# A softmax denominator's constant, its reciprocal and its column of ones: three small moves in a fused attention and soft-MoE kernel

## The chip, the cores and the metric

The kernel runs on one core of one Trainium2 chip. The metric is the device time of one execution in microseconds (us); times of several executions are given by their median. The profile is of one further execution, taken by the hardware profiler.

The engines named below are PE (TensorE, matrix products and transposes), DVE (VectorE), ACT (ScalarE), POOL (GpSimd, which also issues most of the loads) and SP (SyncE, which issues the loads of v and the stores).

## The reference

The first half is attention with one extra term in the softmax denominator, the second a soft mixture of experts on its output. Only the first half matters here:

```python
scores = scale * np.matmul(q, k.transpose(0, 1, 3, 2))
m = np.max(scores, axis=-1, keepdims=True)
e = np.exp(scores - m)
attn = e / (np.sum(e, axis=-1, keepdims=True) + np.exp(-m) + 1e-09)
return np.matmul(attn, v).astype(np.float32)
```

There are 8 batches, 12 heads, 448 positions and 64 numbers per head. `np.exp(-m)` is the sink term, one number for each row of scores, and `1e-09` the constant of this document's title. The result, with the heads laid side by side, is the input `x` (3584 x 768) of the mixture: logits `x @ phi`, a softmax over the rows for the slots' inputs, two layers of weights per expert, and a softmax over the slots to mix their outputs back into every row.

## The kernel before, in words

The attention is cut into 24 **units**, u = 0 to 23; a unit is two batches by two heads (a head pair), and six units make up one pair of batches. A unit is worked in 7 **steps** of 64 positions. Everything is placed on one clock of steps, n = 7u + s: a function `at(n, where, f)` (L679) notes what is to be issued at step n, and the loop at L726 issues it. Within a step the order is: what is noted as "small", the score tile of step n, "value", the transposed score tile of step n - 10, "end", "load". The program is issued in exactly this order, engine by engine; nothing reorders it later. Each engine works through its own list in order and waits on semaphores for what others make.

What a unit does, with its place on the clock (n = 7u):

- `stage_S` (L220), steps n to n + 6: PE writes a score tile into PSUM (L226, in the last step L230) and DVE takes its row maxima (L234, 128 x 896 numbers). These reductions fill most of DVE's time.
- `stage_T` (L208), step n + 5: PE transposes q and k of the next unit, DVE copies them out (L217).
- `stage_MT` (L236), step n + 7: the maxima are transposed on PE (L238), copied by ACT (L240), ACT makes the sink terms `em` (L242), and POOL writes the maxima in the form that PE can subtract, in two parts (L246, L252).
- `stage_ST` (L257), steps n + 10 to n + 16: PE makes the transposed scores with the maxima subtracted (L262, L267), ACT the exponential (L271).
- `stage_V` (L274), step n + 9: POOL converts v to bf16 (L276) and writes a 1.0 beside each value (L278), so that the product with v also yields the row sums. The target is one of two buffers, by the parity of u.
- `stage_AV` (L281), steps n + 13 to n + 18: PE multiplies with v (L297). `stage_AVout`, step n + 19: ACT copies the product out (L308, L311) into `xu`, of which there is one buffer.
- `stage_den` (L314), step n + 20: POOL adds row sum and sink term (L317) and then 1e-9 (L318).
- `stage_N` (L321), step n + 22, "small": DVE takes the reciprocal (L324), POOL multiplies (L326). For u = 22 it is step n + 21 and both are on DVE; unit 23 has a function of its own, `stage_last`, that adds its own 1e-9.
- `stage_X` (L369), step n + 26: PE transposes the result (L378), DVE copies it out (L379).

So the reciprocal of unit u stands in DVE's list between the first and the second reduction of unit u + 3 (steps 0 and 1 of that unit). In the same stretch POOL's list has: the loads of q and k (L124, four DMAs) and of weights (L155, one DMA, in units 9, 13 and 16 two), issued at step 5 of a unit; L317 and L318 at step 6; L246 and L252 at step 7, which is step 0 of the next unit; L326 at its step 1; L276 and L278 at its step 2. `mixture` (L391) puts further work between, once per six units: among it POOL's subtraction `gate_max` (L487), which waits for DVE, and its multiplication `gate_out` (L499).

Score tiles, transposed score tiles and all transposes share one ring of three PSUM slots (`slot`, L115; 496 tiles in all). A tile usually takes the slot that was taken three tiles ago, and PE waits until its reader, DVE or ACT, is done with it. So the transposed score tile of a step usually waits for DVE's reduction of the step before, and a score tile for ACT's exponential two steps back. At three places the build gives a transposed score tile the slot of the transposed score tile of the step before, two tiles back: in unit 10 at its steps 2 and 3 and in unit 14 at its step 2, counted by the score tiles that are made then.

Of the kernel before, what the change touches and what calls it, by code (L numbers as in the profile page):

```python
# [13 lines left out]
ALU = mybir.AluOpType  # L14
# [9 lines left out]
def kernel(  # L24
# [10 lines left out]
    nc = tc.nc  # L35

    B, H, S, D = q.shape
# [10 lines left out]
    U = BP * HP  # L48
# [9 lines left out]
    small = ctx.enter_context(tc.tile_pool(name="small", bufs=2))  # L58
# [30 lines left out]
    def buf(name, i):  # L89
        o, n, bufs = parts[name]  # L90
        return block[:, ds(o + (i % bufs) * n, n)]

    def xbuf(u):
        return block[:, ds(xbuf_at((u + 4) % (HP + 1)), N2)]
# [20 lines left out]
    def slot(shape, dtype=F32):  # L115
        return ring.tile(shape, dtype, tag="r", name="ps")
# [11 lines left out]
    def load_qk(u):  # L128

        for i, (src, name) in enumerate(((q, "qr"), (k, "kr"))):  # L130
            t_ = buf(name, 0) if u else wres[:, WRES - 1, ts(i, N2)]
            RAW[u, name] = load(u, t_.rearrange("p (h n) -> p h n", h=2), src, nc.gpsimd)

    def load_v(u):
        t_ = block[:, ds(parts["vr" if u < U - 1 else "qr"][0], 2 * N2)].bitcast(F32).rearrange("p (h n) -> p h n", h=2)
        RAW[u, "vr"] = load(u, t_, v, nc.sync if u else nc.gpsimd)
# [71 lines left out]
    def stage_T(u, name):  # L208

        ps = slot([128, 2, S], BF16)  # L210
        r = RAW.pop((u, name))
        for t in range(TB):
            for h in range(2):
                nc.tensor.transpose(ps[ds(h * D, D), :, ds(t * P, P)],  # L214
                                    r[:, h, ds(t * D, D)], ident)
        t_ = buf(f"qk{u % 3}", 0)[:, ts(int(name == "kr"), N2)].rearrange("p (b n) -> p b n", b=2)
        nc.vector.tensor_copy(t_, ps)  # L217
        (QT if name == "qr" else KT)[u] = t_
# [17 lines left out]
    def stage_MT(u):  # L236
        ps = slot([128, 128], BF16)
        nc.tensor.transpose(ps, M[u % 2], ident)  # L238
        mt = small.tile([128, 128], BF16, tag="mt", name="mt", bufs=1)
        (nc.scalar.copy if u < U - 1 else nc.vector.tensor_copy)(mt, ps)  # L240
        em = small.tile([128, 2, TB], F32, tag="em", name="em", bufs=3)
        nc.scalar.activation(em, M[u % 2].rearrange("p (h r) -> p h r", h=2)[:, :, ds(0, TB)],  # L242
                             AF.Exp, scale=-scale)
        EM[u] = em
        md = buf(f"md{u % 2}", 0).rearrange("p (b n) -> p b n", b=2)
        nc.gpsimd.tensor_tensor(  # L246
            md[:, :, ds(0, C3 * 128)].rearrange("p b (c n) -> p b c n", c=C3),
            mt.unsqueeze(1).unsqueeze(1).broadcast_to([128, 2, C3, 128]),
            nmask[:, ds(0, 2 * C3)].rearrange("p (b c) -> p b c", b=2).unsqueeze(3)
                 .broadcast_to([128, 2, C3, 128]),  # L250
            op=ALU.mult)
        nc.gpsimd.tensor_tensor(  # L252
            md[:, :, ds(C3 * 128, P)], mt.rearrange("p (b n) -> p b n", b=2),
            nmask[:, ds(2 * C3, 1)].unsqueeze(2).broadcast_to([128, 2, P]), op=ALU.mult)
        MD[u] = md

    def stage_ST(u, t):  # L257
        ps = slot([128, 2, 512])
        for b in range(2):
            for h in range(2):  # L260
                hs = ds(h * D, D)
                nc.tensor.matmul(ps[ds(b * P, P), h, ds(0, S)], ones[hs, :], MD[u][hs, b, :],  # L262
                                 start=True, stop=False)
        for b in range(2):
            for h in range(2):
                hs = ds(h * D, D)
                nc.tensor.matmul(ps[ds(b * P, P), h, ds(0, S)],  # L267
                                 KT[u][hs, b, ds(t * P, P)], QT[u][hs, b, :],
                                 start=False, stop=True)
        et = buf("et", u * TB + t).rearrange("p (h n) -> p h n", h=2)  # L270
        nc.scalar.activation(et, ps[:, :, ds(0, S)], AF.Exp, scale=scale)  # L271
        ET[u, t] = et

    def stage_V(u):  # L274
        t_ = buf(f"v6{5 + u % 2}", 0).rearrange("p (h t e) -> p h t e", h=2, e=66)
        nc.gpsimd.tensor_copy(t_[:, :, :, ds(0, D)],  # L276
                              RAW.pop((u, "vr")).rearrange("p h (t d) -> p h t d", t=TB))
        nc.gpsimd.memset(t_[:, :, :, ds(D, 1)], 1.0)  # L278
        V65[u] = t_

    def stage_AV(u, ts_, part):  # L281

        for t in ts_:
            if t == 0 and part == 0:
                AV[u] = pav.tile([128, 2, 512], F32, tag="av", name="av")
            av, et = AV[u], ET[u, t]
            for h in range(2):
                for c in (range(C3) if part == 0 else (C3,)):  # L290
                    for b in range(2):
                        bs = ds(b * P, P)
                        if c < C3:
                            o, w = av[:, b, ds((h * C3 + c) * 65, 65)], 128
                        else:
                            o, w = av[bs, h, ds(2 * C3 * 65, 65)], P
                        nc.tensor.matmul(o, et[bs, h, ds(c * 128, w)],  # L297
                                         V65[u][bs, h, t, ds(0, 65)],
                                         start=(t == 0 and h == 0 and c == 0),
                                         stop=(t == TB - 1), skip_group_check=True)  # L300
            if part == 1:
                ET.pop((u, t))

    def stage_AVout(u):
        av = AV.pop(u)
        xu = buf("xu", 0).bitcast(F32).rearrange("p (h s e) -> p h s e", h=2, e=65)
        copy = nc.scalar.copy if u < U - 2 else nc.vector.tensor_copy
        copy(  # L308
            xu[:, :, ds(0, 2 * C3), :].rearrange("p h (b c) e -> p b h (c e)", b=2),
            av[:, :, ds(0, 2 * C3 * 65)].rearrange("p b (h e) -> p b h e", h=2))  # L310
        copy(xu[:, :, TB - 1, :], av[:, :, ds(2 * C3 * 65, 65)])  # L311
        XU[u] = xu

    def stage_den(u):  # L314
        xu = XU[u]
        den = small.tile([128, 2, TB], F32, tag="den", name="den")
        nc.gpsimd.tensor_tensor(den, xu[:, :, :, D], EM.pop(u), op=ALU.add)  # L317
        nc.gpsimd.tensor_scalar(den, den, 1e-9, None, op0=ALU.add)  # L318
        DEN[u] = den

    def stage_N(u):  # L321
        xv = XU.pop(u)
        rec = small.tile([128, 2, TB], F32, tag="rec", name="rec", bufs=1)
        nc.vector.reciprocal(rec, DEN.pop(u))  # L324
        x = xbuf(u).rearrange("p (s n) -> p s n", s=TB)
        (nc.gpsimd if u < U - 2 else nc.vector).tensor_tensor(  # L326
            x.rearrange("p s (h d) -> p h s d", h=2), xv[:, :, :, ds(0, D)],
            rec.unsqueeze(3).broadcast_to([128, 2, TB, D]), op=ALU.mult)
        X[u] = x
# [349 lines left out]
    def at(n, where, f):  # L679
        plan.setdefault((n, where), []).append(f)  # L680

    for u in range(U):
        n = u * TB
        if u + 1 < U:
            at(n + 5, "value", lambda u=u: [stage_T(u + 1, name) for name in ("qr", "kr")])
        if u + 2 < U:
            at(n + 5, "load", lambda u=u: load_qk(u + 2))
        at(n + 7, "value" if u < U - 1 else "small", lambda u=u: stage_MT(u))
        at(n + (9 if u < U - 1 else 5), "load", lambda u=u: stage_V(u))
        if u + 1 < U:  # L690
            at(n + (9 if u < U - 2 else 5), "load", lambda u=u: load_v(u + 1))
        for m in sorted(set(AV0)):
            at(n + m, "value", lambda u=u, m=m: [
                stage_AV(u, [t for t in range(TB) if AV0[t] == m], part) for part in range(2)])
        if u < U - 1:
            at(n + 19, "small", lambda u=u: stage_AVout(u))
            at(n + 20, "value", lambda u=u: stage_den(u))
            at(n + (22 if u < U - 2 else 21), "small", lambda u=u: stage_N(u))
        else:
            at(n + 11, "load", lambda u=u: last_sinks(u))  # L700
            at(n + 19, "small", lambda u=u: stage_last(u))
        if u < U - 2:
            at(n + 26, "value", lambda u=u: stage_X(u))
        else:
            at(n + (24 if u == U - 2 else 26), "end", lambda u=u: stage_X(u))
# [135 lines left out]
```

## Time and profile before

| | us |
|---|---|
| median of 3 runs | 329.68 (328.95 to 329.85) |
| the profiled execution | 328.66 |
| its span, first to last instruction | 326.8 |
| PE busy | 283.3 (87%) |
| DVE busy | 255.7 (78%) |
| ACT busy | 213.5 (65%) |
| POOL busy | 211.7 (65%) |
| L324, reciprocal on DVE, 23 times | 0.241 each |
| L318, add of 1e-9 on POOL, 23 times | 0.253 each |
| L317, sum and sink term on POOL, 23 times | 0.276 each |
| L278, ones on POOL, 24 times | 0.160 each |

The profile's page gives for each engine the time in which it had an instruction under way. Its lists by line say how long an engine sat idle ahead of a group of instructions and what ended the wait. The timeline gives starts and durations; a line with "x5" merges five instructions of the same kind that follow each other. Starts on one engine may be closer together than one duration, since instructions overlap at their ends. The chain of waits goes back from the last instruction, at each step to whatever released it.

Times of single steps in what follows are microseconds from the start of the span.

### The profile page before, as it was taken

The numbers are of one execution on the slowest core, as the hardware profiler recorded it, in microseconds if no ns is written. First come the engines' busy times: TensorE is split into PE (matmuls) and PEld (weight loads), VectorE is DVE, ScalarE is ACT, GpSimd is POOL, SyncE is SP. The second block draws the span as 40 slices with busy tenths as digits, with TensorE's granted clock in tenths as the row PEclk, the third lists the DMA queues.
The fourth block names the chain that finished last, engine by engine and source line by source line (L and its number), as shares of the span: only waits on it lengthen the run. The fifth ranks groups of instructions, "written<-read, shape, count | busy, mean of one in ns | idle before, by whom it ended". The sixth has DMA issues, their size and how long they took to land.

```text
span 326.8 us, 13095 instructions
## 1 busy us (share of the span) xinstructions
PE 283.3 (87%) x5794; PEld 160.1 (49%) x5794; DVE 255.7 (78%) x353; ACT 213.5 (65%) x341; POOL 211.7 (65%) x332
## 2 busy tenths in 40 slices
PE   1669999999999899999999998979999897997920
PEld 1325565655565555555555565545555454452300
DVE  1888999998999888988999898868998844516720
ACT  3025877877878677877787787866877884226610
POOL 8256678798787877798868876957875873220000
PEclk9999999999999999999999999997999999898555
DMA  6554788999798799999998899977878699976997
GB/s 87 88 90 83 131 174 163 195 171 173 152 189 161 132 214 187 180 164 172 202 217 140 161 209 222 188 132 157 143 137 165 146 183 208 214 154 244 398 398 308
DMA packets 30311, 59.08 MB, mean 181 GB/s; under 512 B 4048, under 2 KB 22736, under 8 KB 30256
## 3 DMA queue, kind: packets, MB, share of 16 engines
q0 software_dynamic: 19344, 36.69, 65.7%
q1 hardware_dynamic: 10912, 21.57, 20.0%
q8 instruction: 45, 0.74, 0.9%
q14 instruction: 10, 0.08, 0.1%
HBM read 83.46 MB, written 11.01 MB: 289 GB/s over the span
## 4 chain that ended last, share of the span: by engine, by line
PE 62%; DVE 12%; POOL 9%; ACT 7%; issue 5%; DMA 1%; ACTq 0%; POOLq 0%
PE av L297 14%; PE ps L262 11%; PE ps L226 10%; PE ps L267 8%; DVE m L234 6%; ACT block L271 6%; PE ps L214 5%; PE ps L805 4%; PE ps L230 2%; POOL block L246 2%; POOL block L124 2%; PE ps L748 2%; PE ps L644 2%; DVE block L217 2%; POOL block L326 1%
## 5 line engine op out<-in xcount | busy, mean ns | idle before, releaser
L234 DVE TENSOR_REDUCE m<-ps 128x2 bf16<-128x896 f32 x168 | 180.8, 1093 | 18.6 <-PE ps L226 13.7
L271 ACT ACTIVATE block<-ps 128x896 bf16<-128x896 f32 x168 | 153.7, 917 | 56.5 <-PE ps L267 52.7
L297 PE MATMUL av<-block 64*128 64x65 bf16 (+1 forms) x2688 | 83.5, 193 | 1.4 <-issue 1.0
L297 PEld LDWEIGHTS <-block 64*128 64x128 bf16 (+1 forms) x2688 | 70.7, 97 | 27.6 <-issue 9.8
L262 PE MATMUL ps<-block,ones 64*64 64x448 bf16 x672 | 69.7, 369 | 6.6 <-DVE m L234 2.8
L267 PE MATMUL ps<-block 64*64 64x448 bf16 x672 | 67.1, 355 | 0.4 <-issue 0.4
L226 PE MATMUL ps<-block 64*128 64x448 bf16 x288 | 54.5, 374 | 3.1 <-DVE m L234 1.3
L124 POOL DMA_DIRECT2D block<-in_q_dram x46 | 29.5, 644 | 34.7 <-PE ps L214 34.7
L226 PEld LDWEIGHTS <-block 64*128 64x128 bf16 x288 | 19.4, 94 | 52.5 <-issue 51.9
L246 POOL TENSOR_TENSOR block<-mt,nmask 128x768 bf16<-128x768 bf16 x24 | 35.2, 1465 | 8.5 <-ACT mt L240 6.3
L326 POOL TENSOR_TENSOR block<-block,rec 128x896 bf16<-128x896 f32 x22 | 37.1, 1685 | 0.0
L262 PEld LDWEIGHTS <-ones 64*64 64x64 bf16 x672 | 25.5, 106 | 12.2 <-issue 6.9
L217 DVE COPY block<-ps 128x896 bf16<-128x896 bf16 x48 | 27.7, 614 | 2.7 <-PE ps L214 2.7
L124 POOL DMA_DIRECT2D block<-in_k_dram x46 | 27.9, 627 | 2.2 <-PE ps L238 2.2
L214 PE MATMUL ps<-ident,block 128*64 128x128 bf16 x644 | 25.4, 228 | 2.5 <-DVE m L234 0.4
L214 PEld LDWEIGHTS <-block 128*64 128x64 bf16 x644 | 23.0, 114 | 5.6 <-issue 2.0
L267 PEld LDWEIGHTS <-block 64*64 64x64 bf16 x672 | 24.6, 107 | 1.1 <-issue 1.1
L276 POOL CAST block<-block 128x896 bf16<-128x896 f32 x24 | 22.2, 927 | 1.5 <-DMA block<-in_v_dram 1.5
L308 ACT COPY block<-av 128x780 f32<-128x780 f32 x22 | 17.7, 803 | 0.0
L378 PE MATMUL ps<-ident,block 128*128 128x128 bf16 x168 | 13.6, 222 | 3.5 <-DVE block L361 1.5
L240 ACT COPY mt<-ps 128x128 bf16<-128x128 bf16 x23 | 6.1, 266 | 15.6 <-PE ps L238 14.7
L378 PEld LDWEIGHTS <-block 128*128 128x128 bf16 x168 | 11.1, 99 | 8.0 <-issue 2.8
(144 smaller groups left out, 258.8 us busy)
## 6 DMA issues: line engine op xcount, KB each, us to landing
wres<-in_moe_w_dram POOLq DMA_DIRECT2D x24, 768.0 KB, 9.3
out_dram<-wres SPq DMA_DIRECT2D x28, 384.0 KB, 4.2
block<-in_v_dram SPq DMA_DIRECT2D x46, 224.0 KB, 4.5
block<-in_moe_w_dram POOLq DMA_DIRECT2D x8, 768.0 KB, 8.8
block<-in_q_dram POOLq DMA_DIRECT2D x46, 112.0 KB, 3.9
block<-in_k_dram POOLq DMA_DIRECT2D x46, 112.0 KB, 4.5
block<-in_v_dram POOLq DMA_DIRECT2D x2, 224.0 KB, 4.7
wres<-in_q_dram POOLq DMA_DIRECT2D x2, 112.0 KB, 2.9
```

The source lines that it names most:

```text
L124: eng.dma_start(out=t_[ds(b * P, P), :, :], in_=src[bp * 2 + b, ds(hp * 2, 2)].rearrange("h (p t) d -> p h (t d)", t=TB))
L214: nc.tensor.transpose(ps[ds(h * D, D), :, ds(t * P, P)], r[:, h, ds(t * D, D)], ident)
L217: nc.vector.tensor_copy(t_, ps)
L226: nc.tensor.matmul(ps[:, h, ds(0, S)], QT[u][hs, b, ds(c * 128, 128)], KT[u][hs, b, :], start=True, stop=True)
L234: nc.vector.tensor_reduce(m[:, :, s], ps[:, :, ds(0, S)], axis=AX.X, op=ALU.max)
L246: nc.gpsimd.tensor_tensor(md[:, :, ds(0, C3 * 128)].rearrange("p b (c n) -> p b c n", c=C3), mt.unsqueeze(1).unsqueeze(1).broadcast_to([12 ...
L262: nc.tensor.matmul(ps[ds(b * P, P), h, ds(0, S)], ones[hs, :], MD[u][hs, b, :], start=True, stop=False)
L267: nc.tensor.matmul(ps[ds(b * P, P), h, ds(0, S)], KT[u][hs, b, ds(t * P, P)], QT[u][hs, b, :], start=False, stop=True)
L271: nc.scalar.activation(et, ps[:, :, ds(0, S)], AF.Exp, scale=scale)
L297: nc.tensor.matmul(o, et[bs, h, ds(c * 128, w)], V65[u][bs, h, t, ds(0, 65)], start=(t == 0 and h == 0 and c == 0), stop=(t == TB - 1), sk ...
L326: (nc.gpsimd if u < U - 2 else nc.vector).tensor_tensor(x.rearrange("p s (h d) -> p h s d", h=2), xv[:, :, :, ds(0, D)], rec.unsqueeze(3). ...
L378: nc.tensor.transpose(ps[:, ts(s - a, 128)], X[u][:, s, :], ident)
```

## The change

It has three parts:

1. The 1e-9 is no longer added to the denominator. It is added, also on POOL, to the sink terms as soon as these are made: in `stage_MT`, behind L252, thirteen steps earlier on the clock. There are as many instructions as before (units 0 to 22).
2. Reciprocal and multiplication of a unit are issued one step later, at n + 23 in place of n + 22, for units 0 to 20. Units 21 (n + 22) and 22 (n + 21) stay.
3. The ones beside the values are written for units 0 and 1 only, that is once for each of the two buffers; 22 instructions are dropped.

```diff
@@ stage_MT
         MD[u] = md
+        if u < U - 1:
+            nc.gpsimd.tensor_scalar(em, em, 1e-9, None, op0=ALU.add)
@@ stage_V
-        nc.gpsimd.memset(t_[:, :, :, ds(D, 1)], 1.0)
+        if u < 2:
+            nc.gpsimd.memset(t_[:, :, :, ds(D, 1)], 1.0)
@@ stage_den
         nc.gpsimd.tensor_tensor(den, xu[:, :, :, D], EM.pop(u), op=ALU.add)
-        nc.gpsimd.tensor_scalar(den, den, 1e-9, None, op0=ALU.add)
         DEN[u] = den
@@ the plan
-            at(n + (22 if u < U - 2 else 21), "small", lambda u=u: stage_N(u))
+            at(n + (23 if u < U - 3 else 22 if u < U - 2 else 21), "small", lambda u=u: stage_N(u))
```

In the built program the lists of ACT and SP are the same as before. On PE the instructions and their order are the same, but the ring's choice of slots differs: the three short turns in units 10 and 14 are gone, and these transposed score tiles wait for DVE's reduction like the others. On DVE each reciprocal of units 0 to 20 now stands between the second and the third reduction of unit u + 3; in units 9, 15 and 21, where the mixture's own maximum (L429, or L431 and L432) stands there too, it comes behind that. On POOL the new add stands between L252 and L326, and in units 10, 16 and 22 `gate_out` (L499) now comes ahead of L326 and no longer behind it.

## Prediction

> **What bounds the kernel now.** I read the page first: busy times, slices, chain; then who waited for whom on DVE, then DVE's, PE's and POOL's timelines unit by unit.
>
> ```profile
> PE 283.3 (87%) x5794; PEld 160.1 (49%) x5794; DVE 255.7 (78%) x353; ACT 213.5 (65%) x341; POOL 211.7 (65%) x332
> ...
> PE 62%; DVE 12%; POOL 9%; ACT 7%; issue 5%; DMA 1%; ACTq 0%; POOLq 0%
> ```
>
> The chain runs through PE for 62% of the span, through DVE for 12%, POOL 9%. So a shorter DVE or POOL list pays only where PE is seen waiting for it. The change touches one DVE wait, in DVE's list of waits:
>
> ```profile
> DVE m L234 <- PE ps L226: 13.7, 31, 0.9
> DVE rec L324 <- POOL den L318: 6.2, 10, 2.4
> ```
>
> Ten of 23 reciprocals stood 6.2 us in all for POOL's denominator. That is no gain yet. DVE's timeline shows three kinds of units:
>
> ```profile
> 57.62 1.10 DVE L234 TENSOR_REDUCE m<-ps 128x2 bf16<-128x896 f32 x1 [0.53 <-PE ps L226]
> 58.63 0.23 DVE L324 RECIPROCAL rec<-den 128x14 f32<-128x14 f32 x1
> 59.17 5.43 DVE L234 TENSOR_REDUCE m<-ps 128x2 bf16<-128x896 f32 x5 [0.31 <-PE ps L226]
> ...
> 150.62 2.31 DVE L234 TENSOR_REDUCE m<-ps 128x2 bf16<-128x896 f32 x2
> 153.78 0.24 DVE L324 RECIPROCAL rec<-den 128x14 f32<-128x14 f32 x1 [0.85 <-POOL den L318]
> 153.94 5.37 DVE L234 TENSOR_REDUCE m<-ps 128x2 bf16<-128x896 f32 x5
> ...
> 214.83 2.31 DVE L234 TENSOR_REDUCE m<-ps 128x2 bf16<-128x896 f32 x2
> 219.55 0.24 DVE L324 RECIPROCAL rec<-den 128x14 f32<-128x14 f32 x1 [2.42 <-POOL den L318]
> ```
>
> In most units (5 is shown first) the reciprocal lies in a pause in which DVE waits for PE anyway. In six units it waits 0.20 to 0.34, and the reduction behind it still starts within 0.08 of PE finishing its tile (unit 4: tile 48.63 + 0.36, reduction 49.06): nothing lost. Long waits: unit 14 (0.85, two weight DMAs ahead on POOL), unit 10 (0.87, same cause), units 16 and 22 (0.28 each, all DVE-bound there), unit 20 (2.42). I measure what a unit loses from its second score tile to its result transposes (L378): 4.81 in unit 4 (48.63 to 53.44), 5.34 in unit 14 (152.98 to 158.32), 5.84 in unit 10, 5.08 in 16 and 22, 7.62 in 20.
>
> **Part 1, reciprocal one step later: what it gives.** The denominator gets about 1.07 more (one step) plus the 0.33 of L318, so only unit 20 still waits for it.
>
> Unit 14 loses 0.53 against unit 4, partly to the short ring turn there (PE waits 0.35 for ACT at 155.11); both causes go. Gain **0.53**.
>
> Units 10, 16 and 22 meet the next limit, POOL, because `gate_out` now stands ahead of the multiplication and the added constant too:
>
> ```profile
> 175.71 0.29 POOL L317 TENSOR_TENSOR den<-block,em 128x14 f32<-128x14 f32 x1
> 176.09 0.25 POOL L318 TENSOR_SCALAR den<-den 128x14 f32<-128x14 f32 x1
> 176.43 1.47 POOL L246 TENSOR_TENSOR block<-mt,nmask 128x768 bf16<-128x768 bf16 x1
> 177.97 0.40 POOL L252 TENSOR_TENSOR block<-mt,nmask 128x128 bf16<-128x128 bf16 x1
> 178.33 1.69 POOL L326 TENSOR_TENSOR block<-block,rec 128x896 bf16<-128x896 f32 x1
> 179.98 0.61 POOL L499 TENSOR_TENSOR d_sb<-lc,sm 128x256 bf16<-128x256 f32 x1
> ```
>
> Read the starts as a ladder. Without L318, L246 starts at 176.09, L252 1.54 later (177.63), the new add 0.36 later (177.99), L499 some 0.30 later (178.29), L326 0.56 later (178.85), and it ends at 180.54. The result transposes started at 180.83; now they may at 180.6: 0.23 each in units 16 and 22, **0.46**. In unit 10 the same ladder from 111.38 ends the multiplication at 116.21, against 116.72: **0.47**, though DVE and ring alone would give back 1.0.
>
> Unit 20: POOL stood 2.15 us ahead of its k load, for a reason that the profile does not show (it names a PE transpose long done), and PE then waited:
>
> ```profile
> 220.80 0.38 PE L262 MATMUL ps<-block,ones 64*64 64x448 bf16 x4 [1.83 <-DVE m L234]
> ```
>
> After the change the second reduction runs at 217.6 and that tile starts on time at 218.74. The next transposed tile (221.79 before) then needs the third reduction, which waits for the denominator (L317 ends 219.18, plus 0.04, 0.16 and 1.09: 220.5), and POOL's L252, 0.33 sooner than 221.54: 221.25. Gain **0.5**, if the POOL stall comes again. Bounds: 0 to the unit's whole loss, 2.8.
>
> The stall has a second price. The busy time of each engine in one stretch, and behind it the granted clock of PE, DMA share and GB/s:
>
> ```profile
> 222.00:226.00 4.00, 4.00 (x59) 1.94 (x50) 2.98 (x4) 2.80 (x4) 2.22 (x3) 0.57 0.69 143
> ```
>
> The granted clock was 0.57 over 222 to 226, right behind the 1.83 pause; from 221.79 on the unit took 3.02 where unit 4 took 2.18, 0.84 more. A PE pause of 1.6 stays after the change (219.63 to 221.25), so I let the half clock come again. The Trainium skill (TensorE: Matmul & The Clock Gate, What's actually happening) has the clock halved only after a whole idle window of about 3.4 us. By that rule neither pause would do it, and the gain of unit 20 would be 1.3; the trace disagrees, since half clock follows 1.83 here.
>
> **Part 1: what it costs.** The reciprocal leaves a pause and enters a dense stretch. DVE today goes from second to third reduction in 1.05 (59.17 to 60.22, a PE pace; DVE's own pace, where PE is ahead, is 0.94, 176.54 to 177.48). With a reciprocal between it needs 1.01 (57.62 to 58.63) and 0.16 (153.78 to 153.94): 1.17, so the third reduction starts 0.12 late. The transposed tile that waits for it starts 1.18 after it (60.22, 61.40); the shortest such distance in the trace is 1.09 (219.71 to 220.80). That leaves 0.09 slack, 0.03 lost; over the units the slack is 0.06 to 0.17. DVE gains the rest back within the unit (0.94 against 1.09). 21 units at 0.03: **-0.6**. Bounds 0 and 21 x 0.12 = 2.5. PE stays dense, so the cover for all this is that slack alone.
>
> The multiplication does not wait for it: rec ready about 1.65 after the second score tile (unit 4: 50.3), POOL gets to L326 at 50.8.
>
> **Part 2, the constant sooner.** 23 x 0.253 on POOL leave the road to the reciprocal and come back between L252 and L326; L246 starts up to 0.33 sooner, L326 about when it did, or 0.3 later where L246 waits for ACT (unit 5: 58.67 behind a copy ending at 58.59). Result transposes stand at least 0.47 behind L326 in ordinary units (unit 19), and the units near that (13, 19) gain the 0.33 ahead of L246: **0**; without that cover at most 0.3 in the nine or so such units, 2.7. The end of the attention has POOL in the chain (L246 at 261.94, its copy ready at 261.56); PE's own pause there is 0.12 (267.21 to 267.33): **0.1**, bounds 0 and 0.3.
>
> **Part 3, ones.** 22 x 0.160 = 3.5 of POOL, directly ahead of a wait for PE's transposes (L124, 34.7 idle in 19 cases) or, in three units, for DVE's maximum (L487, 7.0 in 3): **0**. If that wait were gone, up to 0.16 a unit.
>
> **Sum.** 0.53 + 0.47 + 0.46 + 0.5 + 0.1 - 0.6 = 1.46 gained. The profiled execution took 328.66, span 326.8 and 1.86 around it: 327.2. The median, 329.68, lies 1.02 above; the same gain gives **328.2**. A measurement of this kernel tells about 0.3%, 1.0 us, from no change.
>
> **Rivals.**
>
> *No unexplained POOL stall in the run* that replaces 2.15 at 217. Then unit 20 gives 2.8, not 0.5: 325.9. For it: nothing in POOL's list demands it. Against: the median of before is above the profiled run, so its runs hold stalls too. 0.20.
>
> *Nothing to see.* PE is the bound, and the slack covers less than I think: a mean of 0.07 lost over 21 units takes 1.5 and leaves 0.1: 329.6. For it: the 62% of PE in the chain. 0.22.
>
> *Slower: the reciprocal takes its whole slot in the dense stretch.* If it starts only when the reduction is out (1.10) and holds DVE for 0.24, the step is 1.34, 0.29 late, 0.20 past the slack: 4.2 over 21 units against 2.1 of gains: 331.8. From 0.15 lost per unit on, the sum is slower than no change by the bound. Against it: reductions of 1.04 start 0.94 apart, and the reduction behind a 0.24 reciprocal starts after 0.16. The Trainium skill (VectorE: DVE Perf Modes, Terms) says that a flush follows every DVE op and the next can't issue until the pipe is empty. By that rule this rival would hold; these overlapping records speak against it, though they may be ends of writes. 0.13.
>
> My forecast: 0.45. Part of its spread (unit 20 giving 0, or a cost of 1.0) falls within 0.3%. Chances: faster by over 0.3% 0.55, within 0.3% 0.30, slower 0.15. Range: down to the rival without stall, 325.8; up to most of the cost's bound with the gains kept, 330.2.
>
> **What would show it.** DVE's wait at the reciprocal gone but for one unit; third reduction 0.10 to 0.15 after its tile rather than 0.04; second score tile to result transposes: 4.81 to 4.87 in units 4 and 14, 4.85 in 16 and 22, 5.4 in 10. L252 about 0.33 sooner in units with a late POOL. Wrong, if ordinary units grow by 0.1 or more, if L378 waits for L326, or if a new stall on POOL or PE appears elsewhere.

## The result and the profile after

The change is faster: by 1.2% here and by 0.7% on another occasion, where 0.45% was predicted. The first interval leaves the predicted ratio out, the second has it in.

| | us |
|---|---|
| before, median of 22 executions | 330.81 (326.35 to 335.35) |
| after, median of 22 executions | 326.29 (323.42 to 330.84) |
| after / before | 0.9883, 95% interval 0.985 to 0.9916 |
| the same kernel on another occasion (below) | 0.993, 0.9893 to 0.9966 |
| predicted | 328.2 against 329.68: 0.9955 |
| profiled execution, before and after | 328.66 and 325.94 |
| its span | 326.8 and 324.0 |

Ratios leave out executions in which the clock or the time was disturbed, medians do not, so the two need not agree to the last digit.

The page after, busy times and the chain of waits:

```profile
PE 280.0 (86%) x5793; PEld 159.0 (49%) x5794; DVE 253.9 (78%) x353; ACT 213.7 (66%) x341; POOL 208.8 (64%) x310
...
PE 54%; DVE 15%; POOL 8%; DMA 8%; issue 5%; ACT 5%; SPq 0%; POOLq 0%; ACTq 0%; DVEq 0%
```

POOL has 22 instructions fewer and PE is busy 3.3 us less for the same work. In DVE's list of waits the reciprocal's (6.2 us in 10 cases before) has shrunk to:

```profile
DVE rec L326 <- POOL den L320: 0.8, 2, 0.6
```

DVE's timeline after (start, duration, instruction, wait ahead of it), units 5, 14 and 20:

```profile
58.47 1.10 DVE L234 TENSOR_REDUCE m<-ps 128x2 bf16<-128x896 f32 x1 [0.46 <-PE ps L226]
59.47 0.23 DVE L326 RECIPROCAL rec<-den 128x14 f32<-128x14 f32 x1
59.62 4.27 DVE L234 TENSOR_REDUCE m<-ps 128x2 bf16<-128x896 f32 x4
...
151.93 1.10 DVE L234 TENSOR_REDUCE m<-ps 128x2 bf16<-128x896 f32 x1 [0.46 <-PE ps L226]
152.94 0.23 DVE L326 RECIPROCAL rec<-den 128x14 f32<-128x14 f32 x1
153.08 4.27 DVE L234 TENSOR_REDUCE m<-ps 128x2 bf16<-128x896 f32 x4
...
217.37 0.24 DVE L326 RECIPROCAL rec<-den 128x14 f32<-128x14 f32 x1 [0.56 <-POOL den L320]
217.53 2.02 DVE L234 TENSOR_REDUCE m<-ps 128x2 bf16<-128x896 f32 x2
```

Unit 14 now looks like unit 5: the reciprocal lies behind the second reduction (listed first) and nothing waits for POOL. Of the units of attention only 20 still does, for 0.56 in place of 2.42; the other wait of the two, 0.19, stands behind the last unit.

POOL's row of work in unit 16, and PE's result transposes behind it:

```profile
174.22 1.52 POOL L246 TENSOR_TENSOR block<-mt,nmask 128x768 bf16<-128x768 bf16 x1
175.82 0.40 POOL L252 TENSOR_TENSOR block<-mt,nmask 128x128 bf16<-128x128 bf16 x1
176.31 0.25 POOL L257 TENSOR_SCALAR em<-em 128x14 f32<-128x14 f32 x1
176.64 0.61 POOL L501 TENSOR_TENSOR d_sb<-lc,sm 128x256 bf16<-128x256 f32 x1
177.21 1.69 POOL L328 TENSOR_TENSOR block<-block,rec 128x896 bf16<-128x896 f32 x1
```

```profile
178.96 0.56 PE L380 MATMUL ps<-ident,block 128*128 128x128 bf16 x7 [0.20 <-POOL block L328]
```

The multiplication (L328) ends at 178.90 and the transposes start 0.06 behind it: POOL bounds the transposes of this unit now (whether it bounds the whole unit is tried further down).

**Where the time went.** From the second score tile of a unit to that of the next, five units differ by the change: unit 10 11.77 to 10.97, unit 14 10.64 to 10.14, unit 16 10.91 to 10.67, unit 20 13.15 to 11.44, unit 22 10.92 to 10.67: **3.50** in all. Ordinary units are unchanged (9.72 and 10.14); unit 21 grows by 0.04 (11.86, 11.90), as it does in every kernel below that has the reciprocal's step. Unit 23 has its second score tile 3.80 sooner (253.11, 249.31); the other 0.30 is the balance of pauses that fall elsewhere (0.71 gained ahead of unit 3, whose place scatters by 1.4 over all the kernels of this study). From there to the end of the span it took 73.6 before and 74.7 after, so 2.75 is left; in the other profiles of this study that use the same code there, this stretch was 74.1 to 77.0, so the profile before had a lucky end, and nothing shows that the change lengthens it.

### The profile page after: what moved, and what is told of

Its sections match the earlier page's. It is cut to its first block, busy times and chain, and to the rows that moved or that the text cites. A ratio compares the mean times of both kernels' runs of the same rounds, so it can differ in the third digit from the quotient of the medians.

```text
span 324.0 us, 13072 instructions
## 1 busy us (share of the span) xinstructions
PE 280.0 (86%) x5793; PEld 159.0 (49%) x5794; DVE 253.9 (78%) x353; ACT 213.7 (66%) x341; POOL 208.8 (64%) x310
## 4 chain that ended last, share of the span: by engine, by line
PE 54%; DVE 15%; POOL 8%; DMA 8%; issue 5%; ACT 5%; SPq 0%; POOLq 0%; ACTq 0%; DVEq 0%
PE av L300 13%; PE ps L264 10%; PE ps L226 9%; DVE m L234 8%; PE ps L269 7%; PE ps L214 5%; ACT block L273 4%; DMA block<-in_moe_w_dram 4%; PE ps L807 3%; DMA block<-in_v_dram 3%; POOL block L328 2%; DVE block L217 2%; PE ps L230 2%; POOL block L246 2%; PE ps L412 1%
## 5 line engine op out<-in xcount | busy, mean ns | idle before, releaser
L269 PE MATMUL ps<-block 64*64 64x448 bf16 x672 | 66.0, 353 | 0.0
L246 POOL TENSOR_TENSOR block<-mt,nmask 128x768 bf16<-128x768 bf16 x24 | 35.7, 1489 | 8.4 <-ACT mt L240 7.1
L328 POOL TENSOR_TENSOR block<-block,rec 128x896 bf16<-128x896 f32 x22 | 37.2, 1689 | 1.4
L264 PEld LDWEIGHTS <-ones 64*64 64x64 bf16 x672 | 24.7, 105 | 10.1 <-issue 4.8
L240 ACT COPY mt<-ps 128x128 bf16<-128x128 bf16 x23 | 6.1, 266 | 15.2 <-PE ps L238 14.5
```

What stands on the lines that cost most here:

```text
L246: nc.gpsimd.tensor_tensor(md[:, :, ds(0, C3 * 128)].rearrange("p b (c n) -> p b c n", c=C3), mt.unsqueeze(1).unsqueeze(1).broadcast_to([12 ...
L269: nc.tensor.matmul(ps[ds(b * P, P), h, ds(0, S)], KT[u][hs, b, ds(t * P, P)], QT[u][hs, b, :], start=False, stop=True)
L328: (nc.gpsimd if u < U - 2 else nc.vector).tensor_tensor(x.rearrange("p s (h d) -> p h s d", h=2), xv[:, :, :, ds(0, D)], rec.unsqueeze(3). ...
```

## The experiments

### One part alone, and one part left out

Three kernels with one part each: the reciprocal's step, the constant, the ones.

```diff
# rec_only
-at(n + (22 if u < U - 2 else 21), "small", lambda u=u: stage_N(u))
+at(n + (23 if u < U - 3 else 22 if u < U - 2 else 21), "small", lambda u=u: stage_N(u))
# const_only: stage_den and stage_MT
-nc.gpsimd.tensor_scalar(den, den, 1e-9, None, op0=ALU.add)
+if u < U - 1:
+    nc.gpsimd.tensor_scalar(em, em, 1e-9, None, op0=ALU.add)
# ones_only
+if u < 2:
     nc.gpsimd.memset(t_[:, :, :, ds(D, 1)], 1.0)
```

> The reciprocal one step later, nothing else of the change. Theory A (the reciprocal's step carries the change): the waits of DVE behind L318 go, unit 14 gains 0.5, unit 10 0.4, units 16 and 22 0.2 each, unit 20 1.5 if POOL's stall of 2.15 recurs, and the dense stretch costs nothing: 2.8 to 3.9 us faster than before, ratio 0.988 to 0.9915, as the whole change (0.9883). Third reduction 0.13 to 0.16 after its tile, ordinary units 4.78 to 4.81. Rival B (a shorter POOL list carries a large part; the 0.7 gained before unit 3 and the 0.4 to 0.5 gained in units 6, 10 and 11 are POOL's): ratio 0.993 to 0.996. Rival C (the step pays only because the constant has left the path to the denominator): ratio 0.994 or more, and DVE still waits for L318 in several units.

> The constant added to the sink terms in stage_MT, nothing else of the change. The denominator is ready 0.33 sooner. Theory A: a partial substitute for the reciprocal's step, since it shortens the same wait: unit 14 gains up to 0.33, unit 10 0.3, units 16 and 22 0.2 each, unit 20 0.3; 1.0 to 1.5 us faster, ratio 0.9955 to 0.997; DVE's wait at the reciprocal falls from 6.2 to about 3. Rival B (the added constant ahead of the multiplication costs as much as it gives): ratio 0.999 to 1.001. Rival C (it is the constant that carries the change): ratio 0.990 or less.

> The ones written for two units only, nothing else of the change. Theory A: the 22 x 0.16 on POOL stand directly ahead of waits and are worth nothing: ratio 0.997 to 1.003, each unit as before to 0.05 but for stalls that the profile puts down to issue. Rival B (the shorter POOL list carries a large part of the change): ratio 0.996 or less, with the start of unit 3 up to 0.7 sooner and units 6, 10 and 11 up to 0.5 shorter.

And the change with one of these hunks taken back: no_rec, no_const, no_ones.

> The changed kernel with the reciprocal where it was (constant and ones changed). Theory A: the sum of the two single parts, 1.0 to 1.5 us faster than before, ratio 0.9955 to 0.997, so two thirds of the gain is lost. Rival B (the shorter POOL list): ratio 0.991 to 0.993. Rival C (the constant carries the change): 0.990 or less.

> The changed kernel with the constant where it was (reciprocal and ones changed). With the single parts measured (reciprocal 0.9871, constant 0.9876, ones 0.9965, constant and ones 0.9967, all 0.9883) the parts are not a sum. Theory A (reciprocal's step and constant shorten the same wait, either gives nearly all, the ones nothing; per unit the step gives 0.4 to 0.5 in unit 14, 0.8 in unit 10, 0.2 each in 16 and 22): ratio 0.987 to 0.991. Rival B (the builds differ by something other than the three edits, such as where PE's own pauses fall, and single ratios scatter by 0.4%): a ratio anywhere in 0.987 to 0.997, and only means over builds tell.

> The changed kernel with the ones written for every unit (reciprocal and constant changed). Theory A: the ones are worth nothing, so it is as the whole change: ratio 0.985 to 0.990. Rival B (scatter between builds): anywhere in 0.985 to 0.996. Rival C (dropping the ones costs time, as constant and ones against the constant alone would have it, 0.9967 against 0.9876): 0.983 or less.

And the changed kernel itself again, unaltered:

> The changed kernel once more, beside the other two. Theory A (the units show what the edits do, and PE's pauses that the profile puts down to issue fall anywhere): units 14, 16 and 22 as in its first profile to 0.03, unit 10 to 0.1, unit 20 6.0 to 6.2 from second score tile to result transposes, pauses by issue in other units than 8, 11, 15 and 18; ratio 0.985 to 0.9916 as before. Rival B (those pauses belong to the program): the same units have them to 0.1.

Measured: the ratio to before, and from each trace the time from second score tile to the next unit's in the five units; "half" says whether the granted clock fell to 0.50 in unit 20.

| kernel | ratio (95%) | 10 | 14 | 16 | 22 | 20 | half |
|---|---|---|---|---|---|---|---|
| before | 1 | 11.77 | 10.64 | 10.91 | 10.92 | 13.15 | yes |
| ones_only | 0.9965 (0.9928 to 1.0002) | 11.77 | 10.64 | 10.92 | 10.91 | 12.24 | no |
| const_only | 0.9876 (0.9838 to 0.9913) | 11.78 | 10.64 | 10.67 | 10.67 | 11.84 | no |
| no_rec | 0.9967 (0.9927 to 1.0007) | 11.78 | 10.64 | 10.67 | 11.17* | 12.79 | yes |
| rec_only | 0.9871 (0.9819 to 0.9922) | 11.21 | 10.26 | 10.67 | 10.67 | 12.75 | yes |
| no_const | 0.9923 (0.9876 to 0.997) | 11.21 | 10.29 | 10.67 | 11.74* | 11.88 | no |
| no_ones | 0.9866 (0.9796 to 0.9936) | 10.99 | 10.14 | 10.67 | 10.67 | 11.47 | no |
| after | 0.9883 (0.985 to 0.9916) | 10.97 | 10.14 | 10.67 | 10.67 | 11.44 | no |
| after_again | 0.993 (0.9893 to 0.9966) | 10.97 | 10.14 | 10.67 | 10.67 | 11.45 | no |

(* has a pause of PE behind its result transposes that comes and goes.)

The units repeat to 0.03 where the same parts are in, but for half clock and the marked pauses; the ratios do not. The same kernel gave 0.9883 and 0.993, and the constant with ones (0.9967) came out 0.9% above the constant alone (0.9876), of which the two profiled executions show 0.95 us, 0.3%, as half clock in unit 20 and 0.5 us as a pause in unit 22. The rest of that difference stays open. Means over the four kernels with a part against the four without (after_again left out): the reciprocal's step -0.66%, the constant -0.42%, the ones +0.31%, each with about 0.31 either way, worked out from the single intervals as if they were independent. So the first two count, and the ones cannot be told from nothing: Rival B of ones_only, a shorter POOL list, has nothing in the units to stand on.

By its ratio alone, const_only (0.9876) would bear out its Rival C, that the constant carries the change. Its five units gain 1.79 of the 3.50, as those of rec_only gain 1.83, and 0.9 of its 1.79 is that half clock did not come in unit 20.

The units tell more. In 14 only the step helps (0.38 alone, 0.50 with the constant). What held unit 14 was the short turn of the ring more than DVE's wait. The constant alone shortens that wait from 0.85 to 0.51, and still PE stands as long for ACT at the same place, 2.13 behind the second score tile (before, then const_only):

```profile
155.11 0.38 PE L262 MATMUL ps<-block,ones 64*64 64x448 bf16 x4 [0.35 <-ACT block L271]
```

```profile
153.56 0.38 PE L264 MATMUL ps<-block,ones 64*64 64x448 bf16 x4 [0.35 <-ACT block L273]
```

The two pauses for ACT in unit 10 (0.32 and 0.42) are also the same in both kernels. All four kernels without the step have these three pauses to 0.01, and all ten with it have none, so what the step gives in 14 and 10 comes at least in part from the ring's other choice of slots. What it would give with the short turns kept, no run shows.

In 16 and 22 either part gives the full 0.24. In 10 the constant alone gives nothing, on top of the step 0.22. In 20, compared among the rows without half clock (12.24 with neither part), the constant gives 0.40, the step 0.36, both 0.79; half clock costs 0.87 to 0.95 more in the three kernels that have it, each against the kernel with the same parts in this unit. So neither part carries the change; "either gives nearly all" was wrong, and so was Rival C, that the step pays only with the constant.

The second profile of the changed kernel had the pauses elsewhere: unit 8 from second score tile to result transposes 5.36 and then 4.80, unit 18 5.60 and then 4.91, unit 7 4.78 and then 5.17; only unit 15 (5.82, 6.38) and, more weakly, unit 11 (5.21, 5.00) were long both times. With these two exceptions they are noise of an execution, not of the program; in before and no_rec unit 15 has no such pause (5.54, 5.56), in const_only it has one (5.79).

### The reciprocal made twice

```diff
+        if u < U - 3:
+            nc.vector.reciprocal(rec, DEN[u])
         nc.vector.reciprocal(rec, DEN.pop(u))
```

> The changed kernel with the reciprocal of units 0 to 20 made twice in the same place, so that DVE has 0.24 more in the stretch between second and third reduction. Theory A (the reciprocal costs nothing there because a slack of 0.09 covers its 0.08, and the slack is then used up: the transposed tile stands exactly 1.09 behind the second reduction): the second one delays the third reduction's turn by 0.2 in full, the transposed tile behind it too, second score tile to result transposes 4.78 to 4.98, 21 units x 0.2 = 4 us slower than the changed kernel, ratio to before 0.999 to 1.002. Rival B (DVE has room there, its 0.94 against PE's 1.08 pays for anything): as the changed kernel, 0.987 to 0.991, 4.78 to 4.82 in ordinary units.

Measured: 0.9969 (0.9937 to 1.0001). Ordinary units take 4.99 to the result transposes and 9.98 or 10.39 to 10.44 in all, against 4.80, 9.72 and 10.14. Unit 5, DVE from the second reduction on, and the PE tile that waits for the third:

```profile
58.63 1.10 DVE L234 TENSOR_REDUCE m<-ps 128x2 bf16<-128x896 f32 x1 [0.46 <-PE ps L226]
59.64 0.23 DVE L327 RECIPROCAL rec<-den 128x14 f32<-128x14 f32 x1
59.91 0.24 DVE L328 RECIPROCAL rec<-den 128x14 f32<-128x14 f32 x1
60.06 3.10 DVE L234 TENSOR_REDUCE m<-ps 128x2 bf16<-128x896 f32 x3
```

```profile
61.15 0.38 PE L264 MATMUL ps<-block,ones 64*64 64x448 bf16 x4
```

The third reduction now starts 1.43 after the second (58.63 to 60.06), and the tile 1.09 after that, the shortest at which a tile follows the reduction that it waits for in these traces (the first tile of unit 0 apart). With one reciprocal it was 1.15 (58.47 to 59.62) and 1.09 as well (60.71), with none 1.05 and 1.18. So the 1.18 had 0.09 to spare, the first reciprocal takes it and costs nothing, and the second, which makes the third reduction 0.28 later, costs 0.19 up to the result transposes and 0.25 a unit. Theory A held in place and, for the unit, in size; the ratio of 0.9969 lies just below its range of 0.999 to 1.002.

### The weight loads four steps later

```diff
-        at(u * TB + 5, "load", lambda i=i: load_w(i))
+        at(u * TB + 9, "load", lambda i=i: load_w(i))
```

> The changed kernel with the weight loads (L155) of units 2 to 22 issued behind the cast of v, four steps later, so that 0.62 of POOL (1.17 in units 9, 13 and 16) leaves the way from the loads to the multiplication. Theory A (what the changed kernel still loses in units 10, 16, 20 and 22 is POOL's row of work, the result transposes standing 0.06 behind the multiplication): unit 20 loses 0.6 less (6.09 to 5.5), unit 10 0.1 to 0.6, 16 and 22 0.1 each: 0.8 to 1.4 us faster than the changed kernel, ratio to before 0.984 to 0.986. Rival B (POOL's own stall of 2.15 before its 110th DMA grows by what was saved, or the loads collide with those of v): no gain, 0.987 to 0.991.

Measured: 1.0414 (1.0348 to 1.0479), 4.1% slower. Units 10 and 20 did as Theory A said (4.83 and 5.56 to the result transposes), 16 and 22 did not (5.00 and 4.88, against 4.89). But units 11, 15 and 18, the ones behind the doubled loads of 9, 13 and 16, took 15.84, 15.45 and 17.65 where the changed kernel took 10.25, 12.41 and 11.12: 15.2 of the loss. POOL's and PE's waits, and the DMA issues with their size and median time to landing:

```profile
POOL block L278 <- DMA block<-in_v_dram: 21.0, 11, 4.1
```

```profile
PE ps L214 <- DMA block<-in_q_dram: 6.7, 4, 3.1
```

```profile
block<-in_v_dram SPq DMA_DIRECT2D x46, 224.0 KB, 8.5
...
block<-in_q_dram POOLq DMA_DIRECT2D x46, 112.0 KB, 7.9
```

v took 8.5 to land in place of 4.8 and q 7.9 in place of 4.2: the loads collide in their new place. POOL waits 2.7 for v in the changed kernel and 21.0 here, and PE waits for q. Part of the loss is the clock: in each of units 11, 15 and 18 the granted clock fell to 0.50, for 6.83, 3.41 and 6.83. Rival B named the collision but thought it would cancel the gain; it cost more than ten times as much.

### The multiplication ahead of what was put before it

```diff
-            at(n + 9, "end", gate_out)
+            at(n + 10, "value", gate_out)
...
+            at(n + 9, "value", lambda u=u: stage_em(u))
```

Here `stage_em` is the add of 1e-9 to the sink terms, taken out of `stage_MT`.

> The changed kernel with POOL's multiplication put ahead of the two things that stood between: the add of 1e-9 to the sink terms comes behind it (step n + 9), and so does gate_out (step n + 10 of its count). Theory A (what the changed kernel still loses in units 10, 16, 20 and 22 is POOL's row of work ahead of the result transposes): the multiplication starts 0.33 sooner in every unit with a late POOL and 0.9 sooner in units 10, 16 and 22; second score tile to result transposes from 5.43 to 4.85 in unit 10, from 4.89 to 4.83 in 16 and 22, from 6.09 to 5.75 in unit 20: 0.8 to 1.1 faster than the changed kernel, ratio to before 0.984 to 0.987. Rival B (the next limit, DVE or the ring, stands right behind POOL's): unit 10 stays above 5.2, unit 20 above 5.95, ratio as the changed kernel in the same call.

Measured: 0.9876 (0.9819 to 0.9933), median 325.58; after_again beside it 0.993, median 326.38. (The profiled execution took 328.72, with 12.92 in unit 8 in place of 10.14 for a PE pause that the profile puts down to issue, so only its single units are read.) Units 10, 16 and 22 reach their result transposes in 4.83, as Theory A had it, but unit 10 as a whole gains only 0.23 (10.74), since what follows the transposes gets longer (5.91 against 5.55), and 16 and 22 gain nothing (10.67), so there POOL holds the transposes but not the unit. Unit 20 stays (6.23): PE stands there for L252 (1.31, as it does for 1.12 in the changed kernel), which was not moved. It has the lowest median of all kernels here, though the intervals do not tell it from the changed one.

### POOL's stall

Before its 110th DMA, the first k load of unit 20, POOL stood 2.1 to 2.2 us in all twelve profiles up to here. Two kernels were to tell what that is. In the first, one weight load is moved behind it; in the second, built on the multiplication first, three weight loads are split in two and the load of unit 18 comes four steps later.

```diff
# load_moved
-for i, u in enumerate(sorted((*range(2, U - 1), 9, 13, 16))):
+for i, u in enumerate(sorted((*range(2, U - 1), 9, 13, 22))):
# stall_moved
-gdma(out=t_, in_=src)
+for a, b in ((0, 1), (1, J)) if i < 3 else ((0, J),):
+    gdma(out=t_[:, ds(a, b - a)], in_=src[:, ds(a, b - a)])
...
-at(u * TB + 5, "load", lambda i=i: load_w(i))
+at(u * TB + (9 if u == 18 else 5), "load", lambda i=i: load_w(i))
```

> The changed kernel with the second weight load of unit 16 issued in unit 22. It asks what POOL's stall of 2.1 to 2.2 is, which stood ahead of the first k load of unit 20, POOL's 110th DMA, in every kernel so far, with POOL lists of two lengths. Theory A (it belongs to the count of DMAs that POOL has issued): one DMA less before it, so it stands one DMA later, between the two k loads of unit 20. Theory B (to what they carry, bytes or packets): it stands more than one DMA later, at the weight load of unit 20 or in unit 21. Theory C (to a place in the program or to the traffic then): it stays ahead of the first k load or is gone. Time: under A as the changed kernel, 0.986 to 0.991; where the stall is gone, unit 20 gives 1.3 more; unit 16 gives up to 0.3.

> The kernel with the multiplication first, and two edits for POOL's stall: the first three weight loads are each split in two DMAs (three more before it), and the weight load that was POOL's 107th DMA, issued in unit 18 at its step 5, is issued four steps later, behind the cast of v. Theory A (the stall of 2.1 belongs to the 110th DMA that POOL issues): it now stands ahead of that weight load, behind unit 19's multiplication and where POOL mostly waits for PE anyway; unit 20 goes from 6.1 to 6.2 down to 4.8 to 5.0 from second score tile to result transposes, about 1.2 to 1.4 faster than with the multiplication first, ratio to before 0.981 to 0.987. Rival B (the load in its new place meets the loads of v, as all 24 did when they were moved together and cost 4.1%): unit 20 is shorter, but units 18 to 20 lose as much in waits for v, q or k: ratio as with the multiplication first, 0.985 to 0.992. Rival C (the stall is not counted in DMAs): it stays ahead of the first k load of unit 20, 6.1.

POOL's timeline in the changed kernel, then load_moved, then stall_moved:

```profile
215.32 1.20 POOL L124 DMA_DIRECT2D block<-in_k_dram  x2 [2.15 <-PE ps L238]
```

```profile
210.96 0.62 POOL L124 DMA_DIRECT2D block<-in_k_dram  x1
213.57 0.60 POOL L124 DMA_DIRECT2D block<-in_k_dram  x1 [1.99 <-issue]
```

```profile
210.38 0.65 POOL L156 DMA_DIRECT2D wres<-in_moe_w_dram  x1
211.82 1.19 POOL L124 DMA_DIRECT2D block<-in_q_dram  x2 [0.80 <-PE ps L215]
213.00 1.20 POOL L124 DMA_DIRECT2D block<-in_k_dram  x2
```

With one DMA less ahead of it the stall stands between the two k loads, again ahead of the 110th DMA: it goes by the count, as Theory A had it. (The releaser that the profile names differs from kernel to kernel, or is missing, so none of those named explains it.) With three more the 110th should be the weight load at 210.38, and there is no stall there nor at any DMA near it. So the plain count is not the whole rule either. That kernel has two edits, the split and the moved load, and which of them took the stall away is not shown; the cause stays open. What the stall costs can be read: without it unit 20 takes 10.59 and 4.80 to the result transposes, against 11.63 and 6.23 in the kernel that stall_moved was built on, and 11.45 and 6.09 in the changed one.

Times: load_moved 0.9959 (0.9921 to 0.9998), with unit 22, which got the second load, at 12.03 in place of 10.67 (1.26 of it is a pause of PE behind the result transposes, which no_rec, no_const and rec_twice also have, with 0.41 to 0.97, so it is not shown to be the load's) and unit 16, which lost one, at 10.67 as in the changed kernel; that is above the 0.986 to 0.991 of Theory A; stall_moved 0.9873 (0.9814 to 0.9931), median 325.97. The 1.04 of unit 20 does not show against the kernel with the multiplication first: it is 0.3%, inside both intervals.

## Why the prediction was right and where it was wrong

Right in sign and range, too small: 1.46 predicted, 3.50 in the units that the change touches, 0.7% (after_again) to 1.2% in the times. About 0.9 of the 3.50 is a half clock that came in the profile before and not in the one after; that it came before was partly luck, since ones_only stood longer at the same place and did not get it (last section).

**DVE's wait, the third reduction, ordinary units:** as predicted. The wait is gone but for unit 20 and one more, the third reduction starts 0.11 to 0.16 after its tile, ordinary units are unchanged. (Of the ten waits before, five are the short ones in which nothing was lost, not six.)

**Unit 14, 0.53:** measured 0.50, to the transposes 0.53 (5.34 to 4.81). Both causes went together. The short ring turn was the one that ended last: in const_only DVE's wait is 0.34 shorter, PE's pause for ACT stays 0.35, and the unit stays at 10.64. (In before, 1.09 behind the second reduction at 153.94 is 155.03; PE started at 155.11.)

**Units 16 and 22, 0.23 each:** 0.24 and 0.25. The end of the ladder on POOL was right, and the transposes stand 0.06 behind L328 (4.89 to them, said 4.85). Two of its rungs were not, and by luck they cancel: L246 starts 0.18 behind the sum (L320) and not 0.38, and from L246 to the multiplication it takes 2.99 and not 2.76. So L252 comes 0.48 sooner than before, not 0.33. One of the prediction's own signs of being wrong did occur, that the transposes wait for the multiplication: 0.20 in 16 and 22, 0.67 in 10. It contradicts the ladder, by which they had to.

**Unit 10, 0.47:** to the transposes 0.41 (5.84 to 5.43, said 5.4), but 0.80 in all. The step that failed is that I stopped counting at the transposes. While PE waits for POOL there, DVE finishes its reductions: their copy started 1.01 behind them before (116.72, 117.73) and 0.61 now (115.83, 116.44), and the next copies with it. Here, being late for POOL's sake was cheaper than being late with the reductions.

**Unit 20, 0.5:** 1.71, the term of the sum that was mis-sized most. The stall came again (2.15), and the ladder was right: the tile that waits for L252 started at 219.29, which with the 1.88 that the unit starts sooner is 221.17, against my 221.25. Two things behind it were not. "A PE pause of 1.6 stays after the change, so I let the half clock come again": the pause was 1.12 and the clock stayed full, 0.92 gained. And the rest of the unit gave 0.79, not 0.5 (the rows without half clock). The waiting tile in the changed kernel:

```profile
219.29 0.38 PE L264 MATMUL ps<-block,ones 64*64 64x448 bf16 x4 [1.12 <-POOL block L252]
```

The Trainium skill (TensorE: Matmul & The Clock Gate, What's actually happening) would have had no half clock in either kernel, by its rule of a whole idle window. No half clock after is what came, but the rule is not the reason: in before, rec_only and no_rec it came after pauses of 1.53 to 1.83 (last section).

**Cost of the dense stretch, -0.6:** 0, mis-sized. The third reduction came as late as worked out (1.15 to 1.16 behind the second, against 1.17), 0.09 to 0.12 later after its tile than before, and the tile stood at its shortest distance, so all of the slack was used. I charged the difference, 0.03, to each unit; it does not reach the result transposes (4.78 to 4.81 before and after), so it is absorbed within the unit. rec_twice shows that any more is paid nearly in full. That also prices the slower rival: a reciprocal that takes its whole slot would have made the third reduction 0.19 later than it came, against 0.28 for the second one, and would have cost in proportion. The Trainium skill's flush (VectorE: DVE Perf Modes, Terms), by which that rival would hold, does not show as a cost here: the record of the next reduction starts 0.15 after the start of the reciprocal's, which is 0.23 long.

**Part 2 at 0:** its own new place on POOL cost nothing in ordinary units, as said (in unit 10 it is part of what mult_first takes from the way to the transposes), but its use was larger than the text makes it look. I counted it inside the other terms, as the 0.33 that L318 leaves the road; alone it gives 0.24 in 16 and 22 and 0.40 in 20, and left out it costs 0.24 in 10 and 0.15 in 14.

**Part 3 at 0:** not contradicted; +0.31% with 0.31 either way.

**The end, 0.1:** cannot be seen: the stretch from unit 23 on scatters by 3.4.

The rival "no unexplained POOL stall", 325.9, names the nearest time, but not the way: the stall did recur. Without it the unit gives 0.9 to 1.0 more (stall_moved). The rival "nothing to see" was also summed wrongly: the gains of the sum are 2.06, and 1.5 lost leaves 0.6, not 0.1.

## What to carry to other kernels

A wait of one instruction can hold several costs in a row (its own, the ring's, the clock's); take each through the unit to its end, not to the next landmark, and ask of every PE pause whether it pulls the clock down. A small instruction may be moved into a dense stretch as long as the distance to the tile that waits is above its shortest value in the trace: that difference, here 0.09, is what it may cost, and beyond it nearly all of it is paid. Moving a load out of one engine's way puts it into other loads' way: look at the time to landing before moving all of them.

## What the chip showed that I had not expected

**Half clock goes by fixed windows of 3.41 us.** Up to 286 us, stretches at half clock last 3.41 us, or two of these in a row, and their starts in one trace lie whole multiples of 3.41 apart. So the trace can be cut into these windows, and PE's busy time read in each. Below, the window with the pause and the next one (busy time of PE, PEld, DVE, ACT and POOL, then the granted clock, DMA share, GB/s), in before, after, no_rec and const_only:

```profile
218.70:222.10 3.40, 1.57 (x45) 0.84 (x38) 2.55 (x4) 1.19 (x2) 3.15 (x6) 1.00 1.05 165
222.10:225.50 3.40, 3.40 (x43) 1.56 (x35) 2.38 (x3) 2.20 (x4) 2.12 (x3) 0.50 0.64 127
```

```profile
217.50:220.90 3.40, 2.27 (x52) 1.28 (x52) 2.76 (x4) 1.83 (x2) 3.15 (x4) 1.00 1.07 170
220.90:224.30 3.40, 3.25 (x69) 2.22 (x73) 3.36 (x6) 2.56 (x4) 2.75 (x5) 1.00 0.61 118
```

```profile
216.90:220.30 3.40, 1.86 (x43) 0.92 (x39) 2.86 (x4) 1.47 (x2) 3.15 (x6) 1.00 0.98 155
220.30:223.70 3.40, 3.37 (x39) 1.80 (x41) 2.44 (x3) 2.28 (x3) 1.98 (x2) 0.50 0.74 137
```

```profile
216.40:219.80 3.40, 1.86 (x52) 0.99 (x46) 1.64 (x3) 1.61 (x2) 3.32 (x6) 1.00 0.84 117
219.80:223.20 3.40, 3.18 (x65) 1.85 (x62) 3.36 (x4) 2.75 (x4) 3.17 (x5) 1.00 0.90 168
```

PE busy for 1.57 of 3.40: the next window is at 0.50. Busy for 2.27: not. At 1.86 it went one way and the other. Over all fourteen profiles, from 40 to 286 us, 16 of the windows at full clock had PE idle for 1.70 or more, and half clock followed each; 949 had it idle for less than 1.35, and it followed none; of the nine between, it followed four. (Of 22 windows that were at half clock themselves two were followed by another, both in load_late, with PE idle for only 0.58 and 0.92.) The Trainium skill (TensorE: Matmul & The Clock Gate, What's actually happening) has windows of 3413 ns that run freely, and so it is here; it has them idle before the clock falls, and here about half is enough. So a pause of 1.9 can be free if a boundary cuts it: in ones_only PE stood 1.94 and the clock stayed full, since 0.4 of it lay in one window and 1.54 in the next. Whether the half clock, worth 0.9 us, comes in unit 20 is thus partly chance for the kernels that pause there for 1.5 to 1.9. With the 1.12 of the changed kernel the window is idle for 1.13, and no window under 1.35 brought it.

**A stall of POOL of 2.0 to 2.2 us once in 131 DMAs**, ahead of the 110th in thirteen profiles and absent in the kernel that issued 134; what makes it is open.
